# The end of a fused attention and MLP kernel: earlier shuffles, lo parts on GpSimd, and two moved steps in the output projection

## The chip, the cores and the metric

The kernel runs on one core of a Trainium2 chip. The core has a matrix engine (TensorE, PE in the profile, its weight loads PEld), and the vector (VectorE, DVE), scalar (ScalarE, ACT) and general (GpSimd, POOL) engines. SyncE (SP) issues nearly all DMAs. Each engine works through its own queue in order and waits on semaphores of the others. The metric is the device time of one execution, in microseconds (us); lower is better. The kernel before took 707.58 us (median of three runs, 707.07 to 707.70).

## The reference

Two branches are added to the layer-normed input's residual, in float32; S = 2048 tokens, D = 640, F = 1728, 32 heads of 20.

```python
x = A_x
xn = _layernorm(x, axis=-1)
# A: linear attention
qkv = (xn @ wqkv) -> q, k, v per head
phi = lambda t: concat([softmax(t @ w_phi), softmax(-(t @ w_phi))])
kv = einsum("bhsf,bhsd->bhfd", phi(k), v);  z = phi(k) summed over s
o = (phi(q) @ kv) / (phi(q) . z + 1e-6)
A = o.reshape(B, S, D) @ wo
# B: layernorm, Dense(F), GELU, Dense(D)
return x + A + B
```

The last product, `o @ wo`, is what the change touches.

## The kernel before

**Precision.** A float32 operand is split into a hi part (rounded to the matrix engine's float32r) and a lo part (the rest). A product is three matmuls: hi x hi, hi x lo, lo x hi (`mm3`, lines 70 to 72). Hi parts are ACT copies; lo parts are subtractions on DVE or POOL.

**Tiling.** Tokens stand in four blocks of 512 (blocks 0 to 3), the 640 columns in five chunks of 128. A PE product fills one PSUM bank of 128 x 512, and DVE adds it from the bank to the running output (`read`, L1547, and `column`, L1514), which frees the bank.

**Stages.** The first MLP groups, the projections to q, k, v with their features, then the remaining MLP groups with the attention of the four blocks beside them, and last the output projection from about 635 us. That last stage computes block pairs (0, 1) and (2, 3). Part of each pair's output goes through a scheme with seven block products instead of eight. Its operands are, beside the parts themselves, *turned forms* of the activations (differences of parts of the two blocks, `combine`, L1464, numbered (form, half): (1, 0) to (4, 1)) and sums of `wo`'s blocks (`add`, L1443, `hi_sum`, L1446 and L1448, `lo_sum`, L1452). `opened` computes the products that need no turned form, `closed` the rest; `column` computes plain columns.

**What a block needs before it can be projected.** `quotients` loads the attention's reciprocal denominators into `rx` (L1256 to L1261). For each of five chunks DVE spreads them over the partitions (`stream_shuffle`, L1267) and POOL multiplies (L1269). Then `Attention.split` makes the hi part (L1283, ACT), for blocks 0 to 2 also a copy of the value into a PSUM bank (L1286, ACT), and the lo part on DVE: from the bank copy (L1288) or, for block 3, from the SBUF tile in a shuffled view (L1290). A turned form is one POOL subtraction, two ACT copies (L1482: hi part and bank copy) and one DVE subtraction (L1487).

**What sets the order.** The order is written out by hand. Each `mm3` of PE is one tick. `mlp.after(t, step)` puts a step t ticks later into the program, and `quotients` is a generator that goes one `yield` per tick; its loop puts one shuffle every three ticks. So the table `steps` decides where an instruction stands in its engine's queue, and no engine takes a later instruction first. The bank copies of L1286, L1448 and L1482 take banks 3 and 4 in turn.

**Names.** `y0`/`y1` tiles are hi and lo parts of blocks; `acc0` and `acc1` hold the attention results of blocks 2 and 3 at this time; `e`, `ts`, `t10`, `ph` and `w3` hold output columns, and `m0` to `m6`, `rx` and `e` also hi and lo parts of turned forms.

Of the kernel before, what the change touches and what calls it, by code (L numbers as in the profile page):

```python
# [11 lines left out]
ALU = mybir.AluOpType  # L12
# [34 lines left out]
def f(ap):  # L47
    return ap.bitcast(F32)
# [3 lines left out]
def tile_kernel(ctx: ExitStack, tc: tile.TileContext, x, xT, wkT, wqT, wv, wphi, wo, w1, b1, w2, b2,  # L52
                ident, mmask, emask, vsel, out):
    nc = tc.nc
    ctx.enter_context(nc.allow_low_precision(reason="float32 operands are split exactly into float32r parts"))

    def split(hi, lo, src, scale=None, eng=nc.vector, first=nc.scalar):

        if scale is None:
            if first is nc.scalar:  # L60
                nc.scalar.activation(hi, src, AF.Copy)  # L61
            else:
                first.tensor_copy(hi, src)
            eng.tensor_tensor(lo, src, f(hi), op=ALU.subtract)  # L64
        else:
            nc.scalar.activation(hi, src, AF.Copy, scale=scale)
            nc.vector.scalar_tensor_tensor(lo, src, scale, f(hi), op0=ALU.mult, op1=ALU.subtract)
# [111 lines left out]
    def make_y0(half, xbs, ptile):  # L179

        cols = slice(half * 256, half * 256 + 256)
        for c0, n in ((0, 1), (1, 2), (3, 2)):
            ps = ptile()
            for c in range(n):
                for i in range(2):
                    nc.tensor.transpose(ps[:, c * 256 + i * P:c * 256 + (i + 1) * P],
                                        xbs[i][:, (c0 + c) * P:(c0 + c + 1) * P], idt)
            src = ps[:, :n * 256].rearrange("p (c t) -> p c t", c=n)
            cs = slice(c0, c0 + n)
            split(y[0][0][:, cs, cols], y[0][1][:, cs, cols], src)  # L190
            yield
# [27 lines left out]
    class Mlp:  # L219
# [39 lines left out]
        def take_parts(self, c):  # L259

            r1, r2 = self.raw.pop(c)
            w = wp.tile([P, 4, D], F32R, name=f"w{self.slots[c % 4]}")
            w1h, w1l = (w[:, i, :].rearrange("p (c f) -> p c f", f=P) for i in range(2))
            w2h, w2l = w[:, 2, :], w[:, 3, :]

            def last():


                split(w1h[:, :, 0:64], w1h[:, :, 64:128], r1[:, :, 0:64])
                nc.vector.memset(f(w1l[:, :, 64:128]), 0.0)  # L270
                nc.vector.tensor_copy(w1l[:, :, 0:64], f(w1h[:, :, 0:64]))
                nc.scalar.activation(w2h, r2, AF.Copy)
                nc.vector.memset(f(w2l[64:128, :]), 0.0)
                nc.vector.tensor_tensor(w2l[0:64, :], r2[0:64, :], f(w2h[0:64, :]), op=ALU.subtract)

            return (w1h, w1l, w2h, w2l), [last] if c == 13 else [
                lambda: split(w1h, w1l, r1, eng=nc.gpsimd),
                lambda first=nc.scalar, eng=nc.gpsimd: split(w2h, w2l, r2, eng=eng, first=first)]
# [294 lines left out]
    def step(gen, n):  # L573
        for _ in range(n):
            next(gen, None)
# [337 lines left out]
    turn, exps, subs = [0], {}, {}  # L913
# [107 lines left out]
    for t, i in [(t, i) for t in range(14) for i in range(4)] + TAIL:  # L1021
# [25 lines left out]
        if i == 0 and t in (1, 2, 3, 6, 7):  # L1047

            kc = (1, 2, 3, 6, 7).index(t)
            lo = rp.tile([P, D], F32, name="r1")  # L1050
            hi = rp.tile([P, D], F32R, name="r2")
# [114 lines left out]
    class Attention:  # L1166
# [72 lines left out]
        def quotients(self):  # L1239

            den, rden = d_dram[self.b]
            ob, parts = self.ob, [(slice(0, 20), "(q c) t -> q c t", 4), (slice(20, 30), "(q c) t -> q c t", 2)]
            for i, (r, form, q) in enumerate(parts):
                nc.sync.dma_start(den[r].rearrange(form, q=q), ob[30 + i::128 // q])
            dt = ep.tile([P, P], F32, name="dt")
            nc.sync.dma_start(dt, den.rearrange("h (q t) -> (h q) t", q=4))
            for i in range(2):
                nc.sync.dma_start(ob[30 + i::32], o_dram[self.b].rearrange("(q i c) t -> i q c t", i=2, c=KC)[i])
            for i in range(13):
                yield  # L1250
            nc.vector.reciprocal(dt, dt)
            nc.sync.dma_start(rden.rearrange("h (q t) -> (h q) t", q=4), dt)
            for i in range(6):
                yield

            nc.sync.dma_start(rx[0::32], rden[0:20].rearrange(parts[0][1], q=4))  # L1256
            yield
            for o in (0, 32):
                nc.sync.dma_start(rx[o + 1::64], rden[20:30].rearrange(parts[1][1], q=2))
                yield  # L1260
                nc.sync.dma_start(rx[o + 2::64], rden[30:32].unsqueeze(1).to_broadcast([2, KC, 512]))  # L1261
                yield
            for i in range(12):
                yield
            for c in range(KC + 1):
                if c < KC:
                    nc.vector.stream_shuffle(rx[:, c, :], rx[:, c, :], SPREAD)  # L1267
                if c:
                    nc.gpsimd.tensor_tensor(ob[:, c - 1, :], ob[:, c - 1, :], rx[:, c - 1, :], op=ALU.mult)  # L1269
                    if self.b < 2:  # L1270
                        nc.sync.dma_start(ob_dram[self.b][:, c - 1], ob[:, c - 1])
                for i in range(3):
                    yield

        def split(self, c, part):

            if (c, part) == (0, 0):
                self.oh, self.ol = (at[self.b - 2].oh, at[self.b - 2].ol) if self.b > 1 else \
                    (yp.tile([P, KC, 512], F32R, name=f"y{p}{self.b % 2}") for p in range(2))
            src = self.ob[:, c].rearrange("p (q t n) -> p t q n", q=4, t=4)  # L1280
            hi, lo = (z[:, c].rearrange("p (t q n) -> p t q n", q=4, t=4) for z in (self.oh, self.ol))
            if part == 0:
                nc.scalar.activation(hi, src, AF.Copy)  # L1283
                if self.b < 3:
                    self.copy[c] = copies()
                    nc.scalar.activation(self.copy[c].rearrange("p (t q n) -> p t q n", q=4, t=4), src, AF.Copy)  # L1286
            elif self.b < 3:
                nc.vector.tensor_tensor(self.ol[:, c], self.copy.pop(c), f(self.oh[:, c]), op=ALU.subtract)  # L1288
            else:
                nc.vector.tensor_tensor(lo, src, f(hi), op=ALU.subtract)  # L1290

    def load_wo():

# [195 lines left out]
    def turn(b0, i, q, *at_):  # L1489
        return [(t, lambda step=step: step(b0, i, q)) for t, step in zip(at_, (combine, turn_hi, turn_lo))]  # L1490

    steps = [(1, load_sums)]
# [1 line left out]
    steps += [(17 + c, lambda c=c: hi_sum(c)) for c in range(4)]  # L1494
    steps += [((57, 19)[k] + c, lambda c=c, k=k: lo_sum(c, k)) for c in range(4) for k in range(2)]
    for n, i, q in ((0, 1, 0), (1, 1, 1), (4, 3, 0), (5, 3, 1), (12, 2, 0), (13, 2, 1), (14, 4, 0), (15, 4, 1)):
        hi = {(1, 0): 6, (1, 1): 15, (3, 0): 8, (3, 1): 10, (2, 0): 23, (2, 1): 25, (4, 0): 27, (4, 1): 29}[i, q]
        steps += turn(0, i, q, n + 1, hi, hi + 1 + (hi > 20))
    for n, (i, q) in enumerate((i, q) for i in (1, 2, 4, 3) for q in range(2)):
        steps += turn(2, i, q, 41 + 2 * n, 44 + 2 * n, 45 + 2 * n)  # L1500
    for n, c, t in [(1, c, 1 + c) for c in range(KC)] + [(2, c, t) for c, t in ((0, 31), (2, 32), (1, 34), (3, 35), (4, 42))] + [(3, c, 61 + c) for c in range(KC)]:
        steps += [(t + part, lambda n=n, c=c, part=part: at[n].split(c, part)) for part in range(2)]
    for t, step in sorted(steps, key=lambda e: e[0]):
# [147 lines left out]
```

## Time and profile before

| | before |
|---|---|
| median of three runs | 707.58 us |
| the profiled execution | 706.55 us |
| its span (first to last instruction) | 704.8 us |
| PE busy | 698.6 us, 99% |
| POOL, ACT, DVE busy | 449.6, 367.7, 525.8 us |
| granted TensorE clock | 1.00 |
| projection, 635 to 705 us: PE busy | 65.5 of 70 us |

All rows below are in microseconds from the start of the span. A timeline row gives start, duration, engine, source line, operation, output and inputs, shape, and in brackets how long the engine was idle before it and what released it. "bank" stands for any bank, and buffer numbers are left out. A matmul's row lasts longer than the distance to the next start, since matmuls are pipelined; PE's pace is therefore read from the starts. A row of stretches gives the length and then busy time and number of instructions of PE, PEld, DVE, ACT and POOL, the granted clock, DMA share and GB/s. A row of one line's instructions gives the shortest, median and longest duration in nanoseconds and the first and last start. A group row ends with total busy time, mean nanoseconds of one, and idle time before them.

### The profile page before, as it was taken

Reading aid. Unit: us, or ns where it says so; the run is one execution under the profiler, and the core shown is the slowest. Engines: PE = TensorE matmul, PEld = TensorE weight load, DVE = VectorE, ACT = ScalarE, POOL = GpSimd, SP = SyncE. Lnnn points to the kernel's source line nnn. Section 1 sums busy time; section 2 is a strip of 40 time slices with the busy share of each in tenths; the row PEclk is TensorE's granted clock in tenths of the full one; section 3 lists DMA queues with packets and bytes.
Section 4 is the critical chain, followed back from the end, with each engine's and each line's share of the span. In section 5 each row is a group of like instructions: output and inputs, shape, how many; then the busy total and the mean of one; then the engine's idle time right before and its main releaser. Section 6 shows DMA issues by size and latency. Waiting matters only on the chain.

```text
span 704.8 us, 9868 instructions
## 1 busy us (share of the span) xinstructions
PE 698.6 (99%) x3363; PEld 588.9 (84%) x3363; DVE 525.8 (75%) x858; ACT 367.7 (52%) x617; POOL 449.6 (64%) x382
## 2 busy tenths in 40 slices
PE   9999999999999999999999999999999999999997
PEld 7888888888888888888888888888888888888786
DVE  7868654877744788788888877747679687787883
ACT  6434643444334545444444546457666657567650
POOL 3711314576245997898787979558689897576630
PEclk9999999999999999999999999999999999999999
DMA  9834633485621227336400608874355649753122
GB/s 323 257 113 128 193 106 99 165 274 168 215 98 75 93 75 238 80 98 204 111 0 17 176 0 315 227 221 124 110 161 168 176 153 302 261 198 132 74 75 104
DMA packets 67463, 107.61 MB, mean 153 GB/s; under 512 B 7622, under 2 KB 31974, under 8 KB 65790
## 3 DMA queue, kind: packets, MB, share of 16 engines
q1 hardware_dynamic: 67110, 106.98, 47.7%
q8 instruction: 26, 0.43, 0.3%
q14 instruction: 23, 0.19, 0.1%
q10 hardware_dynamic: 304, 0.01, 0.0%
HBM read 72.42 MB, written 34.55 MB: 152 GB/s over the span
## 4 chain that ended last, share of the span: by engine, by line
PE 94%; DVE 3%; issue 1%; POOL 1%; ACT 0%; DMA 0%; DVEq 0%; POOLq 0%
PE bank L910 28%; PE bank L70 18%; PE bank L71 18%; PE bank L72 18%; PE bank L980 3%; PE bank L648 2%; PE bank L1218 1%; PE bank L1219 1%; PE bank L554 1%; PE bank L314 1%; PE bank L332 1%; PE bank L313 1%; PE bank L333 1%; PE bank L1150 1%; DVE st L138 0%
## 5 line engine op out<-in xcount | busy, mean ns | idle before, releaser
L910 PE MATMUL bank<-wkh,y 128*128 128x512 f32 (+1 forms) x480 | 139.5, 364 | 0.0
L64 POOL TENSOR_TENSOR w<-r,w 128x640 fp32r<-128x640 f32 x32 | 52.7, 1662 | 93.0 <-ACT w L61 62.5
L70 PE MATMUL bank<-m,w 128*128 128x512 f32 x281 | 110.5, 393 | 0.7 <-DVE t L1547 0.6
L71 PE MATMUL bank<-m,w 128*128 128x512 f32 x281 | 109.4, 389 | 0.0
L70 PE MATMUL bank<-y,w 128*128 128x512 f32 (+1 forms) x264 | 102.7, 389 | 0.1
L72 PE MATMUL bank<-m,w 128*128 128x512 f32 x264 | 102.8, 389 | 0.0
L71 PE MATMUL bank<-y,w 128*128 128x512 f32 (+1 forms) x264 | 102.0, 386 | 0.0
L72 PE MATMUL bank<-y,w 128*128 128x512 f32 (+1 forms) x258 | 99.6, 386 | 0.0
L910 PEld LDWEIGHTS bank<-wkh,y 128*128 128x128 f32 x480 | 87.5, 188 | 13.3
L910 PE MATMUL bank<-wkl,y 128*128 128x512 f32 (+1 forms) x240 | 87.4, 364 | 0.0
L946 ACT ACTIVATE m<-m,rs_all 128x1280 f32<-128x1280 f32 x32 | 43.7, 1364 | 43.6 <-POOL m L945 43.5
L70 PEld LDWEIGHTS bank<-m,w 128*128 128x128 f32 x281 | 52.8, 188 | 12.1 <-DVE t L1547 1.0
L71 PEld LDWEIGHTS bank<-m,w 128*128 128x128 f32 x281 | 52.8, 188 | 10.5
L70 PEld LDWEIGHTS bank<-y,w 128*128 128x128 f32 x264 | 49.6, 188 | 11.0 <-ACT bank L1482 0.5
L948 DVE TENSOR_REDUCE sm<-m 128x64 f32<-128x1280 f32 x32 | 47.4, 1481 | 15.0 <-ACT m L946 14.8
L72 PEld LDWEIGHTS bank<-m,w 128*128 128x128 f32 x264 | 49.6, 188 | 10.4
L71 PEld LDWEIGHTS bank<-y,w 128*128 128x128 f32 x264 | 49.6, 188 | 9.7
L910 PE MATMUL bank<-w,y 128*128 128x512 f32 x240 | 57.4, 391 | 0.0
L72 PEld LDWEIGHTS bank<-y,w 128*128 128x128 f32 x258 | 48.5, 188 | 9.9
L945 POOL TENSOR_TENSOR m<-m,mx 128x640 f32<-128x640 f32 (+2 forms) x48 | 44.5, 941 | 19.2 <-DVE mx L934 19.2
L337 DVE TENSOR_TENSOR acc<-bank,acc 128x512 f32<-128x512 f32 x70 | 47.2, 684 | 12.3 <-PE bank L72 7.0
L910 PEld LDWEIGHTS bank<-w,y 128*128 128x128 f32 x240 | 44.4, 188 | 8.5
(241 smaller groups left out, 1538.9 us busy)
## 6 DMA issues: line engine op xcount, KB each, us to landing
r<-in_w SPq DMA_DIRECT2D x52, 320.0 KB
e<-e SPq DMA_DIRECT2D x40, 256.0 KB
e<-acc SPq DMA_DIRECT2D x52, 160.0 KB
t<-t SPq DMA_DIRECT2D x8, 512.0 KB
acc<-in_xT SPq DMA_DIRECT2D x3, 1280.0 KB
tf<-t SPq DMA_DIRECT2D x2, 1536.0 KB
xb<-in_x SPq DMA_DIRECT2D x8, 320.0 KB
t<-in_x SPq DMA_DIRECT2D x8, 320.0 KB
```

Of the source, the lines that this page charges most:

```text
L64: eng.tensor_tensor(lo, src, f(hi), op=ALU.subtract)
L70: nc.tensor.matmul(ps, lh, rh, start=first, stop=False, **kw)
L71: nc.tensor.matmul(ps, lh, rl, start=False, stop=False, **kw)
L72: nc.tensor.matmul(ps, ll, rh, start=False, stop=last, **kw)
L313: nc.tensor.matmul(pz, w1h[:, kc, :], yh[:, kc, :], start=kc == 0, stop=False)
L337: nc.vector.tensor_tensor(acc[b][:, m, :], pw, acc[b][:, m, :], op=ALU.add)
L648: nc.tensor.matmul(ps[:, u * nh * DF:(u + 1) * nh * DF], raw[:nh * DH, u * P:(u + 1) * P], wpt[:nh * DH, g, :nh, 1:], start=True, stop=True)
L910: nc.tensor.matmul(ps, lh[:, kc, c], rh[:, kc], start=n == 0, stop=n == 3 * KC - 1)
L945: subs[n, t] = nc.gpsimd.tensor_tensor(ep[:, s], a, b, op=ALU.subtract)
L946: exps[n, t] = nc.scalar.activation(e, e, AF.Exp, scale=rs_all[:, t:t + 1])
L948: nc.vector.tensor_reduce(sm, e.rearrange("p s (h f) -> p (s h) f", f=DH), axis=AX, op=ALU.add)
L980: nc.tensor.matmul(kvp[g // 2][:, (g % 2) * 240:(g % 2) * 240 + 240].rearrange("p (s f) -> p s f", s=4), v[:, g * VS:(g + 1) * VS], ft[:, ...
```

## The change

Four edits, all in the output projection's preparation. Block 3's `quotients` yields six times instead of twelve before its shuffles. Block 2's lo parts of chunks 0 to 3 are made by POOL out of the SBUF tile, without the bank copy; chunk 4 stays as it was. The hi part of turned form (1, 1) of blocks 0 and 1 is made at step 21 instead of 15 (its lo part at 23 instead of 16), which puts it behind the sums of `wo`. And the lo parts of the turned forms of blocks 2 and 3 come two steps after their hi parts, not one.

```diff
-            for i in range(12):
+            for i in range(6 if self.b == 3 else 12):
                 yield
...
                 nc.scalar.activation(hi, src, AF.Copy)
-                if self.b < 3:
+                if self.b < 2 or (self.b, c) == (2, 4):
                     self.copy[c] = copies()
                     nc.scalar.activation(self.copy[c].rearrange("p (t q n) -> p t q n", q=4, t=4), src, AF.Copy)
-            elif self.b < 3:
+            elif c in self.copy:
                 nc.vector.tensor_tensor(self.ol[:, c], self.copy.pop(c), f(self.oh[:, c]), op=ALU.subtract)
             else:
-                nc.vector.tensor_tensor(lo, src, f(hi), op=ALU.subtract)
+                (nc.gpsimd if self.b == 2 else nc.vector).tensor_tensor(lo, src, f(hi), op=ALU.subtract)
...
-        hi = {(1, 0): 6, (1, 1): 15, (3, 0): 8, (3, 1): 10, (2, 0): 23, (2, 1): 25, (4, 0): 27, (4, 1): 29}[i, q]
+        hi = {(1, 0): 6, (1, 1): 21, (3, 0): 8, (3, 1): 10, (2, 0): 23, (2, 1): 25, (4, 0): 27, (4, 1): 29}[i, q]
         steps += turn(0, i, q, n + 1, hi, hi + 1 + (hi > 20))
     for n, (i, q) in enumerate((i, q) for i in (1, 2, 4, 3) for q in range(2)):
-        steps += turn(2, i, q, 41 + 2 * n, 44 + 2 * n, 45 + 2 * n)
+        steps += turn(2, i, q, 41 + 2 * n, 44 + 2 * n, 46 + 2 * n)
```

The queues show what that moves. First DVE's queue around the reads of the first products of blocks 0 and 1 (L1547; the numbers tell banks and buffers apart; `y10` is block 2's lo part). Before:

```order
L1547 TENSOR_TENSOR e_5998<-bank1_6285,e_5998 128x512
L1288 TENSOR_TENSOR y10_6019<-bank4_6298,y00_6018 128x512
L1267 STREAM_SHUFFLE rx_4377<-rx_4377 128x512
L1288 TENSOR_TENSOR y10_6019<-bank3_6312,y00_6018 128x512
L1547 TENSOR_TENSOR e_5998<-bank5_6301,e_5998 128x512
L1288 TENSOR_TENSOR y10_6019<-bank4_6319,y00_6018 128x512
L1267 STREAM_SHUFFLE rx_4377<-rx_4377 128x512
L1547 TENSOR_TENSOR ph_6002<-bank2_6323,ph_6002 128x512
L1267 STREAM_SHUFFLE rx_4377<-rx_4377 128x512
L1547 TENSOR_TENSOR t10_6001<-bank1_6285,t10_6001 128x512
```

And the same place now:

```order
L1547 TENSOR_TENSOR e_5998<-bank1_6289,e_5998 128x512
L1267 STREAM_SHUFFLE rx_4377<-rx_4377 128x512
L1547 TENSOR_TENSOR e_5998<-bank5_6301,e_5998 128x512
L1547 TENSOR_TENSOR ph_6002<-bank2_6319,ph_6002 128x512
L1547 TENSOR_TENSOR t10_6001<-bank1_6289,t10_6001 128x512
```

Between the first and the second read of bank 1 the three lo parts (L1288) and two of the three shuffles are gone.

Second, DVE's queue a little further on, where the second read of bank 2 (into `t10`) stands among the lo parts of the turned forms of blocks 2 and 3 (L1487; `m0` belongs to form (1, 0), `m1` to (1, 1), `m2` to (2, 0)). Before:

```order
L1547 TENSOR_TENSOR e_5999<-bank1_6285,e_5999 128x512
L1487 TENSOR_TENSOR m0_6367<-bank4_6368,m0_6367 128x512
L1487 TENSOR_TENSOR m1_6382<-bank3_6383,m1_6382 128x512
L1547 TENSOR_TENSOR t10_6001<-bank2_6323,t10_6001 128x512
L1547 TENSOR_TENSOR ph_6002<-bank1_6285,ph_6002 128x512
L1487 TENSOR_TENSOR m2_6397<-bank4_6398,m2_6397 128x512
```

Now:

```order
L1547 TENSOR_TENSOR e_5999<-bank1_6289,e_5999 128x512
L1487 TENSOR_TENSOR m0_6359<-bank4_6360,m0_6359 128x512
L1547 TENSOR_TENSOR t10_6001<-bank2_6319,t10_6001 128x512
L1487 TENSOR_TENSOR m1_6374<-bank3_6375,m1_6374 128x512
L1547 TENSOR_TENSOR ph_6002<-bank1_6289,ph_6002 128x512
L1487 TENSOR_TENSOR m2_6389<-bank4_6390,m2_6389 128x512
```

Each read stands one lo part further ahead.

Third, POOL's queue over the same time: block 3's multiplications (L1269), block 2's lo parts (L1290), and the turned forms of blocks 2 and 3 (L1464). Before:

```order
L1269 TENSOR_TENSOR acc1_5548<-acc1_5548,rx_4377 128x512 x4
L1464 TENSOR_TENSOR acc0_5166<-acc1_5548,acc0_5166 128x512
L1269 TENSOR_TENSOR acc1_5548<-acc1_5548,rx_4377 128x512
L1464 TENSOR_TENSOR acc0_5166<-acc1_5548,acc0_5166 128x512
L1464 TENSOR_TENSOR e_6377<-acc1_5548,acc0_5166 128x512
```

Now:

```order
L1269 TENSOR_TENSOR acc1_5548<-acc1_5548,rx_4377 128x512 x3
L1290 TENSOR_TENSOR y10_6019<-acc0_5166,y00_6018 128x512 x2
L1269 TENSOR_TENSOR acc1_5548<-acc1_5548,rx_4377 128x512
L1290 TENSOR_TENSOR y10_6019<-acc0_5166,y00_6018 128x512 x2
L1269 TENSOR_TENSOR acc1_5548<-acc1_5548,rx_4377 128x512
L1464 TENSOR_TENSOR acc0_5166<-acc1_5548,acc0_5166 128x512 x2
```

Four lo parts now stand between the multiplications, and the first form (1, 0), which stood ahead of the last multiplication, stands behind all five. SP's queue is the same in both. ACT loses block 2's four bank copies and makes the hi part of form (1, 1) of blocks 0 and 1 after the sums of `wo`.

## The prediction

> **What bounds the kernel.** I read the page's first lines, then who waited for whom on the matrix engine (PE), then busy time by stretch, then the timelines of PE, DVE, POOL, ACT and SyncE's queue (SP) around the one stretch where PE is not full.
>
> ```profile
> span 704.8 us, 9868 instructions
> PE 698.6 (99%) x3363; PEld 588.9 (84%) x3363; DVE 525.8 (75%) x858; ACT 367.7 (52%) x617; POOL 449.6 (64%) x382
> ...
> PE bank L582 <- POOL m L580: 1.3, 1, 1.3
> PE bank L70 <- DVE t L1547: 0.6, 1, 0.6
> ...
> 660.00:673.00 13.00, 12.30 (x54) 9.54 (x53) 11.05 (x20) 7.78 (x15) 11.17 (x9) 1.00 0.22 81
> ```
>
> PE is busy 99% of the span at a granted clock of 1.00 (the third figure from the end). It waits long twice: once at the very start (1.3 us), and once on a DVE read of a bank, L1547. That one lies between 660 and 673 us, in the projection that the change rewrites. A bounded gain therefore comes out of PE's rows there:
>
> ```profile
> 663.96 0.39 PE L72 MATMUL bank<-y,r 128*128 128x512 f32 x1
> 664.90 0.50 PE L70 MATMUL bank<-m,w 128*128 128x512 f32 x1 [0.55 <-DVE t L1547]
> ...
> 668.91 0.39 PE L72 MATMUL bank<-y,r 128*128 128x512 f32 x1
> 669.13 0.39 PE L70 MATMUL bank<-y,w 128*128 128x512 f32 x1
> ...
> 670.27 0.39 PE L72 MATMUL bank<-y,w 128*128 128x512 f32 x1
> 670.80 0.47 PE L70 MATMUL bank<-y,w 128*128 128x512 f32 x1
> ...
> 672.49 0.39 PE L71 MATMUL bank<-y,r 128*128 128x512 f32 x1
> ...
> 697.20 0.39 PE L72 MATMUL bank<-y,r 128*128 128x512 f32 x1
> ```
>
> From 672.49 to 697.20 stand 109 steps from one start to the next: 24.71/109 = 0.2267 us each, PE at its full pace. From 663.96 to 668.91 stand 18 steps, 4.95 us where 18 x 0.2267 = 4.08 would do: **0.87 us lost** (A). From 669.13 to 672.49 stand 13 steps, 3.36 where 2.95 would do: **0.41 us lost** (B). Nothing else is lost from here to the last full column, so 0.87 + 0.41 = 1.28 us is all that PE can give back.
>
> What caused A and B stands on DVE, ACT and POOL:
>
> ```profile
> 660.51 0.68 DVE L1288 TENSOR_TENSOR y<-bank,y 128x512 fp32r<-128x512 f32 x1
> 661.11 0.69 DVE L1547 TENSOR_TENSOR e<-bank,e 128x512 f32<-128x512 f32 x1
> 661.70 0.69 DVE L1288 TENSOR_TENSOR y<-bank,y 128x512 fp32r<-128x512 f32 x1
> ...
> 662.31 0.73 DVE L1267 STREAM_SHUFFLE rx<-rx 128x512 f32<-128x512 f32 x1
> 662.93 0.68 DVE L1547 TENSOR_TENSOR ph<-bank,ph 128x512 f32<-128x512 f32 x1
> ...
> 663.53 0.75 DVE L1267 STREAM_SHUFFLE rx<-rx 128x512 f32<-128x512 f32 x1
> 664.16 0.68 DVE L1547 TENSOR_TENSOR t<-bank,t 128x512 f32<-128x512 f32 x1
> ...
> 669.37 0.69 DVE L1487 TENSOR_TENSOR m<-bank,m 128x512 fp32r<-128x512 f32 x1 [1.49 <-ACT bank L1482]
> 669.98 0.68 DVE L1547 TENSOR_TENSOR t<-bank,t 128x512 f32<-128x512 f32 x1
> ```
>
> A: bank 1's product was complete nine matmuls before 663.96, so its last one began at 661.92 and ended at 662.31. Its read (t<-bank) only began at 664.16, because DVE ran without a break through block 2's lo parts (L1288) and block 3's shuffles (L1267) ahead of it. PE restarts at 664.90, just after the read's end at 664.84. B: the read of bank 2 (669.98) stands behind a lo part of a turned form (L1487) that sat idle 1.49 us for ACT, which had waited for POOL; PE goes on at 670.80.
>
> ```profile
> 647.65 5.07 POOL L1464 TENSOR_TENSOR tf<-tf,tf 128x512 f32<-128x512 f32 x4
> 655.51 2.56 POOL L1269 TENSOR_TENSOR acc<-acc,rx 128x512 f32<-128x512 f32 x2 [2.79 <-DVE rx L1267]
> 660.71 1.29 POOL L1269 TENSOR_TENSOR acc<-acc,rx 128x512 f32<-128x512 f32 x1 [2.64 <-DVE rx L1267]
> 663.12 1.30 POOL L1269 TENSOR_TENSOR acc<-acc,rx 128x512 f32<-128x512 f32 x1 [1.12 <-DVE rx L1267]
> 664.37 1.30 POOL L1464 TENSOR_TENSOR acc<-acc,acc 128x512 f32<-128x512 f32 x1
> ...
> 666.87 1.31 POOL L1464 TENSOR_TENSOR acc<-acc,acc 128x512 f32<-128x512 f32 x1
> ```
>
> POOL sat idle 2.79 + 2.64 + 1.12 = 6.55 us before its multiplications, each time for a shuffle. It then forms turned forms without a break.
>
> **The change, part by part.**
>
> *Four lo parts from DVE to POOL.* The 15 DVE ones are in one group row, and POOL's nearest rows, of the same shape, stand beside it:
>
> ```profile
> L1288 DVE TENSOR_TENSOR y<-bank,y 128x512 fp32r<-128x512 f32 x15 | 9.9, 679 | 0.4 <-ACT bank L1286 0.2
> ...
> L1269 POOL TENSOR_TENSOR acc<-acc,rx x20: 1280/1298/2029, 532.0 to 665.6; 128x512 f32<-128x512 f32 x20
> ...
> L1212 POOL TENSOR_TENSOR e<-e,m x28: 1280/1301/2902, 465.8 to 614.2; 128x512 fp32r<-128x512 f32 x28
> ```
>
> DVE loses 4 x 0.68 = 2.7 us of work ahead of bank 1's read, and ACT four copies into a bank. POOL gains four subtractions that the trace does not show there, with one operand in a shuffled view (runs of 32 elements). Bounds: 1.28 (the fastest contiguous row) to 2.90 us (the slowest). I take 1.30, the median of L1212, because that has the same write type and size and the last run of elements is contiguous. Nothing excludes up to 2.90, so it stays in the range.
>
> *Block 3's shuffles six steps sooner.* A step is three matmuls, 0.68 us, so six are 4.1 us. The five shuffles leave the part of the DVE queue that holds A. Two of them fell right there (662.31, 663.53). The first now stands behind a column's read whose last matmul PE starts 66 matmuls before 663.96, at 649.00, and ends at 649.39. That read takes 0.68 and one half-size lo sum of wo at most as much, so DVE comes to the shuffle between 650.1 and 650.8. It needs the rx loads, which SP issues in the same order as before:
>
> ```profile
> 645.05 0.34 SPq L1515 DMA_DIRECT2D outT<-e  x1
> 645.44 0.54 SPq L1261 DMA_DIRECT2D rx<-d  x1
> ...
> 649.03 0.69 DVE L1487 TENSOR_TENSOR e<-bank,e 128x512 fp32r<-128x512 f32 x1 [2.31 <-DMA outT<-e]
> ```
>
> The transfer issued at 645.05 released DVE at 649.03, 3.98 us later. The last rx load, at that price, lands at 649.4, 0.7 us or more before DVE comes to the shuffle. So it costs nothing; that cover ends if the load takes over 4.7 us. The idle time of 2.31 us in the last row is also what the shuffles fill.
>
> *One turned form behind wo's sums.* Its lo part is the instruction that idled those 2.31 us for a buffer; seven steps (4.8 us) later the buffer is free. PE reads this form from the fourth matmul of the first closed product on, 17 matmuls before 663.96, at 660.1, and the form is done some eight microseconds earlier. It costs nothing, and DVE no longer blocks before 649.03, so wo's sums on DVE come sooner.
>
> *The last lo parts a step later.* Each read of a bank now stands ahead of the lo part that waits for POOL, not behind it: bank 2's read stands behind the lo of turned form (1, 0) instead of (1, 1). This costs DVE nothing.
>
> *POOL's new chain.* It decides B.
>
> ```profile
> 656.91 0.63 ACT L1283 ACTIVATE y<-acc 128x512 fp32r<-128x512 f32 x1 [0.94 <-PE bank L72]
> ...
> 668.75 0.58 ACT L1482 ACTIVATE bank<-acc 128x512 f32<-128x512 f32 x1
> ```
>
> The first lo part needs ACT's hi part, written from 656.91 when PE lets go of the old one, so POOL starts at 657.6; by then its forms (to 652.72) and three multiplications (3 x 1.26 more, 656.5) are done. From 657.6 run, without a break, four lo parts, two multiplications and form (1, 0): seven instructions, 1.26 apart (2.56 - 1.30 in the row at 655.51). Form (1, 0) ends at 657.6 + 6 x 1.26 + 1.30 = 666.46. Before, from the end of a form (666.87 + 1.31 = 668.18) through ACT's two copies, DVE's lo and the read to PE's restart at 670.80 it took 2.62 us. So bank 2 is free at 666.46 + 2.62 = 669.08. PE, without A, wants it six matmuls after 669.13 - 0.87, at 669.62. **Margin 0.54 us**, or 0.13 for each lo part. B is gone, but narrowly. The later forms follow 1.26 apart while PE spends 1.36 on each two-step product, so POOL does not fall back.
>
> Bank 1's read for A: DVE meets it at about 662.4 and ends by 663.1; PE wants it at 663.96 + 0.23 = 664.19, a margin of 1.1.
>
> [...]
>
> ```profile
> 619.44 1.58 POOL L64 TENSOR_TENSOR w<-r,w 128x640 fp32r<-128x640 f32 x1 [0.17 <-ACT w L61]
> 620.02 1.67 DVE L377 TENSOR_TENSOR w<-r,w 64x640 fp32r<-64x640 f32 x1 [0.62 <-ACT w L375]
> 620.97 1.88 POOL L1269 TENSOR_TENSOR acc<-acc,rx 128x512 f32<-128x512 f32 x1
> ```
>
> A DVE subtraction of two SBUF operands took 1.67 us beside a POOL instruction, and the POOL instruction behind it 1.88 instead of 1.30. [...]
>
> **Sum.** The profiled execution took 706.55 us, 1.75 more than its span: 706.55 - 0.87 - 0.41 = 705.27. The median of the runs shown, 707.58, lies 1.03 above it; the same 1.28 off gives **706.3**. That is 0.18%; a change under 0.2% (1.4 us) cannot be told from none here, the three runs alone spanning 0.63.
>
> **Rivals.**
>
> *The lo parts are slow on POOL, and the kernel ends slower.* Each 0.1 us over 1.44 per lo part adds 0.4 us to POOL's chain, form (1, 0), the lo behind it, bank 2's read, and PE. [...] At 2.03 (L1269's slowest) 708.7; at 2.90, 706.3 + 6.4 - 0.54 = 712.2. Slower by over 0.2% (709.0) begins at 2.11 us each. For it speaks that no POOL row shows this view; against it, that all POOL rows of 512 in this stretch took about 1.30. [...]
>
> *A goes, B stays.* Lo parts of 1.5 to 1.6 make PE wait 4 x 0.2 - 0.54 = 0.26 to 4 x 0.3 - 0.54 = 0.66: 706.6 to 707.0; at 1.76 all is given back, and up to 2.11 the time stays under 709.0. The narrow margin speaks for it, the even 1.30 of POOL's rows against it.
>
> *It doesn't do what it says.* The shuffles run only when rx has landed; if that comes at 652 or later, DVE blocks, the reads behind it are late, and A stays: 707.6. The 3.98 us of the neighbouring transfer speak against it.
>
> **How the numbers follow.** Forecast 0.62, B stays (up to 709.0) 0.18, no gain 0.08, POOL slow enough to end above 709.0 0.12. Faster by over 0.2% means below 706.17, only 0.13 under the forecast, which a shift of a run's spread gives in four of ten of the forecast's cases: 0.25. Slower 0.12, and 0.63 for the rest. The range, 705.8 to 708.7, goes from the forecast less most of the runs' spread to lo parts of 2.03 us each and leaves out some 0.07 below and 0.12 above.
>
> **What would show it.** In the profile after: no PE wait on DVE at L1547, and starts 0.2267 apart from 660 to 697; L1290 on POOL four times at about 1.30; POOL's idle time between 652.7 and 666 near 1 us, not 6.55; form (1, 0) ending near 666.5; block 3's first shuffle between 650.1 and 650.8 without a wait for a DMA. I am wrong if L1290 on POOL takes over 1.44 us, if PE waits for bank 2's read near 669.6, or if the shuffle idles for rx.

## The result and the profile after

The changed kernel takes **705.77 us** (median of 21 runs, 705.10 to 707.97), the kernel before, run beside it on the same chip, 707.07 us (21 runs, 706.25 to 708.09). The ratio is 0.9984, with a 95% interval of 0.9978 to 0.9991: 0.16% faster, 1.1 us (0.6 to 1.6), near what can be told from no change at all. The prediction was 706.3 us, counted from the 707.58 us of the runs shown then: a gain of 1.28 us (0.18%). Of all executions here one, of experiment 3, took 1426 us, with PE busy for 1419.4 us where the changed kernel has 698.0; its trace is not read below.

The first lines of the page of the changed kernel's profiled execution (705.84 us), behind them the two longest of PE's waits, and the busy time of the stretch from 660 to 673 us:

```profile
span 704.0 us, 9857 instructions
PE 698.0 (99%) x3363; PEld 588.1 (84%) x3363; DVE 523.6 (74%) x854; ACT 365.8 (52%) x613; POOL 453.6 (64%) x386
...
PE bank L582 <- POOL m L580: 1.3, 1, 1.3
PE bank L186 <- DVE xb L172: 0.5, 1, 0.5
...
660.00:673.00 13.00, 13.00 (x59) 10.76 (x58) 9.07 (x14) 6.73 (x12) 13.00 (x11) 1.00 0.22 81
```

The wait at L1547 is gone from the list, and PE is busy 13.00 of the 13 us in which it was busy 12.30. POOL is full there too. The timeline of DVE in the changed kernel has block 3's first shuffle, the two reads that had been late, and what stands ahead of the second:

```profile
650.74 0.75 DVE L1267 STREAM_SHUFFLE rx<-rx 128x512 f32<-128x512 f32 x1
...
662.71 0.69 DVE L1547 TENSOR_TENSOR t<-bank,t 128x512 f32<-128x512 f32 x1 [0.67 <-PE bank L72]
...
667.97 0.69 DVE L1487 TENSOR_TENSOR m<-bank,m 128x512 fp32r<-128x512 f32 x1 [0.78 <-ACT bank L1482]
668.58 0.68 DVE L1547 TENSOR_TENSOR t<-bank,t 128x512 f32<-128x512 f32 x1
```

The read of bank 1 now waits for PE (0.67 us idle), where PE had waited for it. The read of bank 2 ends at 669.26; PE takes that bank at 669.99. POOL's timeline beside it, and the row of its lo parts in the view of one line:

```profile
652.18 2.56 POOL L1269 TENSOR_TENSOR acc<-acc,rx 128x512 f32<-128x512 f32 x2
655.56 1.29 POOL L1269 TENSOR_TENSOR acc<-acc,rx 128x512 f32<-128x512 f32 x1 [0.82 <-DVE rx L1267]
657.98 2.56 POOL L1290 TENSOR_TENSOR y<-acc,y 128x512 fp32r<-128x512 f32 x2 [1.12 <-ACT y L1283]
...
665.49 2.55 POOL L1464 TENSOR_TENSOR acc<-acc,acc 128x512 f32<-128x512 f32 x2
...
L1290 POOL TENSOR_TENSOR y<-acc,y x4: 1289/1300/1302, 658.0 to 663.0; 128x512 fp32r<-128x512 f32 x4
```

The four lo parts take 1.30 us each, from 657.98 on without a break. PE's starts are 0.2267 us apart from 657.98 to 683.36. One small loss is new, in PE's timeline:

```profile
683.36 0.39 PE L72 MATMUL bank<-y,r 128*128 128x512 f32 x1
683.64 0.47 PE L70 MATMUL bank<-m,w 128*128 128x512 f32 x1
683.95 0.40 PE L71 MATMUL bank<-m,w 128*128 128x512 f32 x1
```

Two steps take 0.59 us instead of 0.45, and with a little after them 0.17 us are lost. From the two traces: A and B give 1.28 back, and this takes 0.17. The two spans differ by less, by 0.74 us; the rest lies outside the change, before 500 us: there this execution loses 0.40 us at 191 and 0.18 at 462, which the kernel before does not, and stands 0.22 ahead by 40 us. 1.28 - 0.17 - 0.40 - 0.18 + 0.22 = 0.75.

### The profile page after: what moved, and what is told of

It is laid out like the page before. It is cut to its first block, busy times and chain, and to the rows that moved or that the text cites. A ratio compares the mean times of both kernels' runs of the same rounds, so it can differ in the third digit from the quotient of the medians.

```text
span 704.0 us, 9857 instructions
## 1 busy us (share of the span) xinstructions
PE 698.0 (99%) x3363; PEld 588.1 (84%) x3363; DVE 523.6 (74%) x854; ACT 365.8 (52%) x613; POOL 453.6 (64%) x386
## 4 chain that ended last, share of the span: by engine, by line
PE 93%; DVE 4%; DMA 1%; issue 1%; ACT 1%; DVEq 0%; ACTq 0%
PE bank L910 28%; PE bank L70 18%; PE bank L71 18%; PE bank L72 18%; PE bank L980 3%; PE bank L648 2%; PE bank L1218 1%; PE bank L1219 1%; PE bank L554 1%; DMA t<-t 1%; PE bank L332 1%; PE bank L333 1%; DVE t L807 1%; PE bank L1150 1%; PE bank L314 0%
```

## The experiments

They ran in three groups (1 to 4, 5 to 8, 9 to 11), each on one chip beside the kernel before (706.64, 706.79 and 706.82 us); a ratio is to the kernel before of the same group, with its 95% interval. The row of the changed kernel is that of the result above, beside 707.07 us. A loss of PE is the time by which its starts between 646 and 696 us exceed 0.2267 us a step, from the profiled execution.

| kernel | median, us | ratio to before | PE's losses, us |
|---|---|---|---|
| before | 706.64 to 706.82 | 1 | 0.87 at 664, 0.41 at 670 |
| changed | 705.77 | 0.9984 (0.9978 to 0.9991) | 0.17 at 684 |
| shuffles alone (1) | 705.35 | 0.9983 (0.9974 to 0.9991) | none |
| lo parts alone (2) | 710.36 | 1.0050 (1.0037 to 1.0063) | 4.87, from 670 on |
| without the lo parts (3, 11) | 705.39, 705.44 | 0.9982 (0.9973 to 0.9991), 0.9981 (0.9972 to 0.9990) | none |
| without the later step (4) | 706.45 | 0.9995 (0.9987 to 1.0004) | 0.76 at 671 |
| without the shuffles (9) | 707.90 | 1.0018 (1.0009 to 1.0027) | 1.32 at 669 to 682, 1.32 from 682 on |
| without the moved form (10) | 705.45 | 0.9980 (0.9971 to 0.9989) | 0.16 at 683 |
| one lo part twice (5) | 707.29 | 1.0006 (0.9997 to 1.0016) | 0.86 at 671, 0.57 at 685 |
| all four lo parts twice (6) | 711.64 | 1.0067 (1.0050 to 1.0084) | 7.02, from 670 on |
| `wo`'s sums later (7) | 705.90 | 0.9985 (0.9976 to 0.9995) | 0.22 at 684 |
| block 3's lo parts in another order (8) | 705.45 | 0.9980 (0.9971 to 0.9990) | none |

**Experiments 1 and 2: one part alone.** The shuffles alone, as an edit of the kernel before:

```diff
-            for i in range(12):
+            for i in range(6 if self.b == 3 else 12):
```

> Only block 3's shuffles are six steps sooner; the lo parts stay on DVE, the moved form and the step stay as before. Theory of the prediction (DVE has to lose the lo parts too): three lo parts of 0.68 us still stand between the two reads of bank 1, so part of the loss A of 0.87 us stays, and B (0.41 us) stays since nothing moves the read of bank 2: gain 0.4 to 0.9 us. Rival (the shuffles alone are the cause): without the shuffles behind the reads DVE has slack, POOL multiplies without waiting and makes form (1, 0) about 4 us sooner, so A and B both go: no PE wait from 655 to 680, gain 1.1 to 1.3 us. Same: no gain, if the lo parts on POOL carry it.

Measured: 0.9983 of before, a gain of 1.2 us (0.6 to 1.8), and PE loses nothing at all from 646 to 696. The rival held, and not the theory, by which part of the losses would stay. Both late reads are early in DVE's timeline:

```profile
661.67 0.69 DVE L1288 TENSOR_TENSOR y<-bank,y 128x512 fp32r<-128x512 f32 x1
662.27 0.69 DVE L1547 TENSOR_TENSOR ph<-bank,ph 128x512 f32<-128x512 f32 x1
662.87 0.69 DVE L1547 TENSOR_TENSOR t<-bank,t 128x512 f32<-128x512 f32 x1
...
668.21 0.68 DVE L1547 TENSOR_TENSOR t<-bank,t 128x512 f32<-128x512 f32 x1
```

The lo parts (L1288) are still here, but without the shuffles between them bank 1's read ends at 663.56, 0.6 us before PE goes on to that bank at 664.16. POOL, whose multiplications now also come sooner, has form (1, 0) done by about 663.2 and DVE has read bank 2 by 668.89, 0.7 us before PE takes it at 669.60. So one edit of the four gives the whole gain.

The lo parts alone:

```diff
-                if self.b < 3:
+                if self.b < 2 or (self.b, c) == (2, 4):
...
-            elif self.b < 3:
+            elif c in self.copy:
...
-                nc.vector.tensor_tensor(lo, src, f(hi), op=ALU.subtract)
+                (nc.gpsimd if self.b == 2 else nc.vector).tensor_tensor(lo, src, f(hi), op=ALU.subtract)
```

> Only block 2's four lo parts go to POOL; shuffles, form and step as before. Theory: POOL still waits for the late shuffles, and four lo parts of 1.28 us now stand ahead of form (1, 0) as well, so A goes (DVE is 2.7 us lighter) but bank 2's read, behind the lo part of form (1, 1), is some 3 us late for PE: net 1.5 to 2.5 us slower than before. Rival (DVE's load is all that counts, POOL has room in its 6.55 us of idle time): A goes and B does not grow, gain about 0.9 us.

Measured: 0.50% slower than before, 3.5 us, where 1.5 to 2.5 was expected. A is gone, but POOL now has late shuffles and four lo parts together, and B grows. PE's timeline around bank 2, and the stretches behind it:

```profile
669.79 0.39 PE L72 MATMUL bank<-y,w 128*128 128x512 f32 x1
673.17 0.47 PE L70 MATMUL bank<-y,w 128*128 128x512 f32 x1 [3.00 <-DVE t L1547]
673.48 0.58 PE L71 MATMUL bank<-y,w 128*128 128x512 f32 x1
673.86 0.63 PE L72 MATMUL bank<-y,w 128*128 128x512 f32 x1
...
676.42 0.63 PE L72 MATMUL bank<-y,r 128*128 128x512 f32 x1
676.85 0.43 PE L70 MATMUL bank<-y,w 128*128 128x512 f32 x1
...
670.00:675.00 5.00, 2.00 (x6) 1.53 (x6) 3.27 (x6) 4.07 (x8) 5.00 (x5) 0.85 0.23 85
675.00:680.00 5.00, 5.00 (x19) 3.96 (x19) 3.92 (x7) 4.62 (x9) 3.00 (x3) 0.81 0.20 73
680.00:685.00 5.00, 5.00 (x24) 4.14 (x23) 4.67 (x10) 1.79 (x4) 0.00 (x0) 1.00 0.14 52
```

Of the 4.87 us, 3.16 are the wait. The rest comes behind it: the matmuls up to 676.85 start 0.38 to 0.43 us apart, nearly twice the usual distance, and the granted clock of the stretches (third figure from the end) is 0.85 and 0.81 before it is 1.00 again. This wait of 3 us cost PE 1.7 us more than its length.

**Experiments 3, 4, 9, 10 and 11: one part undone.** Edits of the changed kernel. First the lo parts back on DVE, shuffles, form and step left as changed:

```diff
-                if self.b < 2 or (self.b, c) == (2, 4):
+                if self.b < 3:
```

> The change without its lo parts on POOL (they stay on DVE with their bank copies). Theory of the prediction: some of A comes back, 0.2 to 0.6 us of PE wait at L1547 near 664, gain 0.7 to 1.0 us. Rival (shuffles and step do it all): PE has no wait between 655 and 680, and form (1, 0) ends about 4 us sooner than in the change, near 661 to 662; gain 1.1 to 1.3 us, the same as the change or 0.1 to 0.2 better.

> The changed kernel with block 2's lo parts back on VectorE once more, for a profile of its own beside the others: shuffles, moved form and later step stay. Theory (the shuffles alone end both losses, so GpSimd's lo parts are not needed): TensorE waits for nothing at 650 to 690, form (1, 0) ends some 4 us sooner than the changed kernel's 666.8, the time is 0 to 0.4 us below the changed kernel's. Rival (VectorE with the lo parts and the shuffles in front of bank 1's read comes late): a wait of 0.2 us or more near 664, the time 0.2 us or more above the changed kernel's.

The two are the same kernel and agree: 0.9982 and 0.9981. In the trace of the second PE loses nothing, and POOL is far ahead: the rival of experiment 3 held. Its timeline, and DVE's reads:

```profile
660.55 1.29 POOL L1269 TENSOR_TENSOR acc<-acc,rx 128x512 f32<-128x512 f32 x1 [2.96 <-ACT y L1283]
661.80 2.54 POOL L1464 TENSOR_TENSOR acc<-acc,acc 128x512 f32<-128x512 f32 x2
...
662.73 0.70 DVE L1547 TENSOR_TENSOR t<-bank,t 128x512 f32<-128x512 f32 x1
664.23 0.69 DVE L1547 TENSOR_TENSOR e<-bank,e 128x512 f32<-128x512 f32 x1 [0.80 <-PE bank L72]
```

Form (1, 0) starts at 661.80 instead of 665.49, and DVE, with the lo parts, is still ahead of PE (idle 0.80 for it). The move of the lo parts to POOL is not needed for either loss.

The last lo parts of the turned forms back at their old step:

```diff
-        steps += turn(2, i, q, 41 + 2 * n, 44 + 2 * n, 46 + 2 * n)
+        steps += turn(2, i, q, 41 + 2 * n, 44 + 2 * n, 45 + 2 * n)
```

> The change with the last lo parts one step after their hi parts again. Theory: bank 2's read stands behind the lo part of form (1, 1), one form (1.26 us) later; the margin of 0.5 to 0.6 us is used up, so PE waits 0.5 to 0.8 us near 670 and B is back: gain 0.4 to 0.7 us against before. Rival (the step does nothing, the sooner forms remove B): no wait there, gain 1.1 us.

B is back, 0.76 us of it, behind the lo part of form (1, 1), which waits for ACT and POOL. DVE's timeline there, and PE's row:

```profile
670.29 0.69 DVE L1487 TENSOR_TENSOR m<-bank,m 128x512 fp32r<-128x512 f32 x1 [0.56 <-ACT bank L1482]
670.90 0.68 DVE L1547 TENSOR_TENSOR t<-bank,t 128x512 f32<-128x512 f32 x1
...
671.72 0.47 PE L70 MATMUL bank<-y,w 128*128 128x512 f32 x1 [0.52 <-DVE t L1547]
```

So the step is needed, but only because the lo parts are on POOL: with the shuffles alone there is no loss without it. This execution also loses about 1 us at 191 and 462, far from the change, so the times and not the span are compared: 0.9995 against 0.9984, 0.8 us. Against the kernel before that is a gain of 0.35 us (-0.3 to 0.9), a little under the expected 0.4 to 0.7 but not to be told from it.

The shuffles back at their old place:

```diff
-            for i in range(6 if self.b == 3 else 12):
+            for i in range(12):
```

> The changed kernel with block 3's shuffles back at their old place; lo parts on GpSimd, moved form and later step stay. Theory (the shuffles' six steps are the part without which the others don't pay: late shuffles come to VectorE and GpSimd just where the lo parts and the forms are now due, so GpSimd's queue ends later): the first loss (0.87 us at about 664) stays away since VectorE has lost block 2's lo parts, but TensorE waits 0.4 to 1.6 us at about 670 to 672.5 and again 0.4 to 0.9 us near 684.7; the sum is 0.8 to 2.2 us against the 1.28 us of the kernel before, so the time is 0.4 us below to 1 us above the kernel before and 0.8 to 2.1 us above the changed kernel. Rival (what the lo parts and the later step take off is enough by itself): no wait over 0.2 us at 664 to 673, the time of the changed kernel within 0.4 us.

Slower than before, by 0.18%. A stays away. The waits at 670 and 673 (0.76 and 0.38) lie in the expected range; those from 680 to 686 add up to 1.34, since DVE stays late for the rest of the stage: 0.95 near 685, where 0.4 to 0.9 was expected, and 0.39 ahead of it, where nothing was. In sum PE loses 2.64 us, above the 2.2 expected, and 1.4 more than the kernel before; by the ratios the time is 1.3 us above the kernel before and 2.4 above the changed one, each a little more than the 1 and the 2.1 expected. POOL's timeline shows why:

```profile
661.55 2.55 POOL L1290 TENSOR_TENSOR y<-acc,y 128x512 fp32r<-128x512 f32 x2
664.05 2.55 POOL L1269 TENSOR_TENSOR acc<-acc,rx 128x512 f32<-128x512 f32 x2
666.54 1.30 POOL L1464 TENSOR_TENSOR acc<-acc,acc 128x512 f32<-128x512 f32 x1
```

Three multiplications, not two, now stand between the first lo part (657.78) and form (1, 0), which starts 8.76 us behind it where the changed kernel has 7.51; a fourth follows, ahead of form (1, 1).

The moved form back (`(1, 1): 15` instead of 21):

> The changed kernel with the turned form (1, 1) of group 0 back in its old place. Theory (with all else in place this form is behind nothing that TensorE waits for): no wait of TensorE at 650 to 680 and the time within 0.3 us of the changed kernel's, of which the 0.17 us at 683.64 may come or go. Rival (the form takes 2.56 us of GpSimd's time ahead of form (1, 0), and the margin at bank 2 is 0.6 to 0.7 us): TensorE waits 1.9 us or more at about 670 and the time is 1.9 to 2.6 us above.

0.9980, no loss but 0.16 us at 683. The form's place makes no difference; the first lo part on POOL still starts when ACT has written its hi part, after 1.47 us of idle time.

**Experiments 5 and 6: the margin.** In the first, block 2's first lo part is done twice on POOL; in the second, all four:

```diff
+                for _ in range(2 if (self.b, c) == (2, 0) else 1):
                     (nc.gpsimd if self.b == 2 else nc.vector).tensor_tensor(lo, src, f(hi), op=ALU.subtract)
```

> The changed kernel with block 2's first lo part (the one whose y is ready at 657.98) done twice on GpSimd, which makes the queue there 1.28 us longer and nothing else. Theory (the margin in front of bank 2's read is what the moved lo parts live on; the trace of the changed kernel puts it at 0.6 to 0.7 us, since DVE ends its read of bank 2 at 669.26 and TensorE takes the bank at 669.99): TensorE waits 0.55 to 0.75 us at about 670, nothing before it, and the time is 0.5 to 0.8 us above the changed kernel's, level with the kernel before within its uncertainty. Rival (GpSimd's 1.94 us of idle time between 652 and 666 take up the second lo part): no wait at 670, the time of the changed kernel.

> The changed kernel with all four of block 2's lo parts that it gave to GpSimd done twice there: 4 x 1.28 = 5.1 us more in front of the turned form (1, 0). Theory (beyond the margin each microsecond of GpSimd's queue comes back whole): TensorE waits 4.2 to 4.8 us at about 670, and what follows a wait that long runs slower for some microseconds, as in the run with block 2's lo parts alone on GpSimd, where the granted clock was 0.90 between 673 and 690 after a wait of 3.2 us: the time is 5 to 7 us above the changed kernel's. Rival (other work of GpSimd moves behind the forms and hides part of it): a wait under 3 us, the time less than 4 us above.

The edit adds a line, so the lines behind it count one more in these two kernels (L1290 is L1291, L1547 is L1548). POOL's lo parts and PE's step to bank 2 with one done twice:

```profile
658.25 3.92 POOL L1291 TENSOR_TENSOR y<-acc,y 128x512 fp32r<-128x512 f32 x3 [1.12 <-ACT y L1283]
...
670.04 0.39 PE L72 MATMUL bank<-y,w 128*128 128x512 f32 x1
671.05 0.47 PE L70 MATMUL bank<-y,w 128*128 128x512 f32 x1 [0.62 <-DVE t L1548]
```

Three subtractions in 3.92 us instead of two in 2.56: POOL's chain is 1.36 us longer. PE's step to bank 2 takes 1.01 us instead of 0.23, a wait of 0.78. The margin is 1.36 - 0.78 = **0.58 us**. DVE stays late behind it and gives PE a second loss, 0.57 us at 685, which was not expected; the time is 0.22% above the changed kernel's (1.5 us), not 0.5 to 0.8. With all four done twice, PE's timeline and the stretch behind the wait:

```profile
669.87 0.39 PE L72 MATMUL bank<-y,w 128*128 128x512 f32 x1
674.92 0.77 PE L70 MATMUL bank<-y,w 128*128 128x512 f32 x1 [4.67 <-DVE t L1548]
...
675.00:680.00 5.00, 5.00 (x13) 3.98 (x14) 3.74 (x7) 4.51 (x9) 5.00 (x5) 0.57 0.29 107
```

The wait is 4.83 us (4.2 to 4.8 expected); with the 0.58 that the margin takes, four more subtractions cost 5.41, 1.35 each. POOL's timeline says the same by itself: from its first lo part (658.08) to form (1, 0) (671.04) it takes 5.45 us more than the changed kernel's 7.51. Beyond the margin POOL's time comes back whole. In the stretch behind the wait, from 675 to 680, the granted clock is 0.57, and PE loses 2.2 us more. Against the changed kernel it is 0.83%, 5.9 us, inside the expected 5 to 7 (the profiled execution, 712.46 us, was the slowest of four).

**Experiments 7 and 8: the new 0.17 us.** In the changed kernel DVE's first `wo` sum beside POOL is stretched. The row of its line in the changed kernel, with the shortest, median and longest of the four in nanoseconds:

```profile
L1452 DVE TENSOR_TENSOR kvs<-w,w x4: 413/416/940, 675.0 to 677.7; 128x256 fp32r<-128x256 f32 x4
```

And in experiment 7, in which these sums come after POOL's last piece (step 60 instead of 57):

```profile
L1452 DVE TENSOR_TENSOR kvs<-w,w x4: 416/417/419, 676.9 to 679.1; 128x256 fp32r<-128x256 f32 x4
```

```diff
-    steps += [((57, 19)[k] + c, lambda c=c, k=k: lo_sum(c, k)) for c in range(4) for k in range(2)]
+    steps += [((60, 19)[k] + c, lambda c=c, k=k: lo_sum(c, k)) for c in range(4) for k in range(2)]
```

> The changed kernel with the four lo parts of wo's sums (L1452, two inputs in SBUF) three steps later, behind the end of GpSimd's last piece at 675.6. Theory (VectorE's instruction with two inputs in SBUF and GpSimd's hold each other up): the four take 0.42 us each, where in the changed kernel the first two took 1.28 us together, and TensorE's 0.17 us at 683.64 is gone: 0.0 to 0.3 us below the changed kernel. Rival 1 (they are stretched by something else, a transfer or ScalarE): they keep 0.6 us for one of the first. Rival 2 (the 0.17 us is not theirs): 0.42 each, but the loss at 683.64 stays.

The stretch of 0.52 us is gone, and the loss at 684 stays (0.22 us), as the second rival said. But what the sums no longer take, DVE spends waiting in its timeline, and the late read comes no sooner for it (683.02, in an execution in which PE runs 0.17 us later):

```profile
675.68 0.69 DVE L1487 TENSOR_TENSOR m<-bank,m 128x512 fp32r<-128x512 f32 x1 [0.49 <-ACT bank L1482]
```

Experiment 8 leaves the sums where they are and orders block 3's lo parts so that the late read stands ahead of them:

```diff
-        steps += [(t + part, lambda n=n, c=c, part=part: at[n].split(c, part)) for part in range(2)]
+        steps += [((({1: 63, 3: 65, 4: 66, 0: 70, 2: 71}[c] if n == 3 else t + 1) if part else t), lambda n=n, c=c, part=part: at[n].split(c, part)) for part in range(2)]
```

> The changed kernel with block 3's lo parts (L1290 on VectorE) in another order, so that the read at 682.82, for which TensorE waited 0.17 us at 683.64, stands ahead of them. Theory (that wait is VectorE's queue): the read comes about 1.2 us sooner and the wait is gone, although the first two L1452 still take about 1.28 us together. Rival (the 0.17 us is TensorE's own, its row names no other engine): it stays at that matmul. Either way the time is within 0.3 us of the changed kernel's.

The read in DVE's timeline of experiment 8, and PE's two steps:

```profile
681.46 0.69 DVE L1547 TENSOR_TENSOR acc<-bank,acc 128x512 f32<-128x512 f32 x1
...
683.30 0.39 PE L70 MATMUL bank<-m,w 128*128 128x512 f32 x1
683.52 0.39 PE L71 MATMUL bank<-m,w 128*128 128x512 f32 x1
```

The read begins at 681.46 (682.82 in the changed kernel), the loss is gone, and the longest L1452 is stretched as it was (925 ns). So another order of DVE's queue is enough to end the loss. Whether the loss would end without the stretch alone is not shown: 0.52 us is more than 0.17, but in experiment 7 a wait of 0.49 us took its place.

None of the kernels is measurably faster than the changed one: those without any loss measure 0.9980 to 0.9983, the changed kernel 0.9984. A simpler kernel, the shuffles alone, does as well as all four edits.

## Why the prediction was right, and where not

*A and B, 0.87 + 0.41 = 1.28 us, and nothing else.* Right: both are gone, the forecast of 706.3 against a measured 0.9984 x 707.58 = 706.4 on the scale of the runs shown then. That the two agree so closely is in part luck, since the interval of the gain is 0.6 to 1.6 us. The sum left out the 0.17 us at 684; it is what a PE that runs ahead meets in a DVE queue that did not move as far: PE is due at that bank at 683.59, where it took it at 684.51 before, and the read ahead of it begins at 682.82, where it began at 683.02. The prediction followed that queue only to the turned forms.

*Lo parts of 1.30 us on POOL.* Right: 1289 to 1302 ns, in the shuffled view too. The bound of 2.90 and with it the slow rival fell. Nor were they stretched as the POOL row of 1.88 us had been: the DVE instructions beside them, from 657.98 to 664.29, were reads of a bank and one shuffle, with one SBUF input each, and kept to 0.69 and 0.75 us. What the prediction did not price is L1452: the one that ran beside POOL, with both inputs in SBUF, took 940 ns, and all four took 416 to 419 when POOL had finished (experiment 7).

*The margin of 0.54 us at bank 2.* Right: 0.58 by experiment 5, with the deciding price of a lo part at 1.30 + 0.58/4 = 1.45 us against 1.44. The prediction's way to it holds also in its parts: form (1, 0) was to end at 666.46, and POOL's row at 665.49 puts the end at about 666.8 in an execution that runs 0.37 us later (bank 2 is taken at 669.99, not 669.62).

*The shuffles find rx landed, and start between 650.1 and 650.8.* Right: 650.74, without a wait for a DMA. The rival that the change does nothing fell with it.

*POOL's idle time near 1 us between 652.7 and 666.* Wrong: 0.82 + 1.12 = 1.94 us. The sum had the first lo part wait for its hi part, but put the three multiplications ahead without a pause; one waited 0.82 us for a shuffle. It cost nothing, since the next instruction waits for ACT anyway.

*DVE loses 2.7 us ahead of bank 1's read.* The amount was right: DVE is busy 2.2 us less, and the 0.52 us of the stretched sum make up the rest. The margin at bank 1 was right too, 1.1 us: its read ends at 663.40, and PE takes the bank at 664.55. But the weight was left open: the prediction never asked which of the two things ahead of the read, lo parts or shuffles, had to go. The shuffles alone leave a margin of 0.6 us there, and one of 0.7 at bank 2 (experiment 1). The lo parts on POOL bring nothing and use up the margin at bank 2, for which the later step then pays. The moved form was priced at nothing, and that is what it is worth.

*The slow rival's price.* It made PE's wait the whole cost. Experiment 6 had 5.2 us more on POOL: 5.2 - 0.54 = 4.66 by that formula, and the wait was 4.83; but with the slower clock behind it PE lost 7.0, and the times say 5.9 above the changed kernel. In experiment 2, with a wait of 3.16 us, the formula is already 1.7 us too low; behind waits of 0.7 to 0.9 us (experiments 4, 5 and 9) there was no slow stretch, the granted clock staying at 1.00.

## What to carry to other kernels

Where one queue is late, find which of the instructions ahead of the late one can go earlier for free, and try that alone first: moving the shuffles, which waited for nothing, gave the whole gain, while moving work onto an engine whose next results are awaited used up a margin that another edit had to buy back. A margin predicted from a chain of rows is worth testing by doing one link twice, and then several: the first run shows the margin, the second the price beyond it. And when the bound engine gets ahead, follow the queues that feed it to the end of the stage, not just to the wait that was removed.

## What the runs showed of the hardware

- **TensorE's clock after a pause.** Behind waits of 0.68, 0.78 and 0.87 us (experiments 4, 5 and 9) the matmuls keep their pace: from the second step on the starts shown are 0.22 to 0.24 us apart, and the granted clock from 660 to 690 is 1.00. Behind the wait with 3.00 us idle (experiment 2) they start 0.38 to 0.43 us apart from 673.48 to 676.85, 3.4 us long, and behind the one with 4.67 us (experiment 6) 0.42 to 0.57 us apart from 674.92 to 679.33, 4.4 us long. In experiment 6 the granted clock falls while PE still waits, from 670.26, where its last matmul ends, to 674.92: its mean is 0.98 from 660 to 673, 0.75 from 670 to 675, 0.57 from 675 to 680 and 1.00 from 680 to 685. A clock of 0.50 from 672.5 to 679.3 gives these means; that is an estimate from them and from the pace, which returns at 679.33. The same estimate for experiment 2, whose means are 0.85 (670 to 675) and 0.81 (675 to 680), is 0.50 from 673.5 to 676.9. By it the low clock lasted 3.4 us in the one and 6.8 in the other, and came 3.3 and 2.2 us after the end of PE's last matmul. No wait between 0.87 and 3.00 us came up in the projection, so it is not shown from which length on the clock falls.
- **VectorE beside GpSimd.** The sum at L1452 with two SBUF inputs that ran beside POOL took 940 ns in the changed kernel and 925 in experiment 8, and 410 to 420 ns where POOL had finished or was about to (changed kernel, kernel before, experiments 1, 7, 8 and 11). Sums of the same line and size that take one input out of a PSUM bank took 406 to 424 ns in the changed kernel between 647 and 652 us, beside POOL's turned forms. So did DVE's subtraction out of a bank at 674.34 (L1487) keep its 0.69 us beside POOL.
- **Scatter far from the change.** At 191 us PE loses 0.40 us in the changed kernel and 0.50 in experiment 4, and nothing in the kernel before and in experiments 1, 2 and 5, kernels that do not differ there; the changed kernel loses 0.18 at 462 as well. A single trace can't be held against another by its span when the question is half a microsecond.
